# A split warm-up, an earlier block of normalisations and an earlier weight load in a fused attention and GEGLU kernel

## The chip, the cores and the metric

The kernel runs on one core of a Trainium2 chip. The core has five engines with a queue of instructions each: PE (TensorE, the matrix multiplier), DVE (VectorE), ACT (ScalarE), POOL (GpSimd) and SP (SyncE), which here only issues transfers (DMAs). Each queue is worked off in order; engines wait for one another through semaphores. The metric is the device time in microseconds; a lower number is better. The time before is 1046.27 us, the median of three runs (1045.1, 1046.27 and 1048.72 us).

## The reference

With x of 2048 tokens by 640 features, in float32:

```python
xn = layernorm(x)                                   # no scale, no bias
qkv = xn @ wqkv                                     # 32 heads of 20
scores = q @ k.T / sqrt(20)                         # causal, window of 256 tokens
A = softmax(scores) @ v @ wo
B = (gelu(xn @ w_gate) * (xn @ w_up)) @ w_down      # inner width 1728
out = x + A + B
```

## The kernel before

All matrix products are made from operands that are split in two: a high part (a copy rounded to the matrix format, made on ACT) and a low part (the rest, a subtraction on DVE or POOL). A product is then three matmuls, high by high, low by high and high by low. So nearly every tile goes through one ACT instruction and one DVE or POOL instruction before PE may use it.

The 2048 tokens are four chunks of 512, each of four tiles of 128 tokens. The work has these stages.

*Start* (lines 434 to 469). x is loaded a tile at a time (`ln_load`, L144, 320 KB each). DVE takes mean and variance (`ln_stats`, L149 to L151), makes the reciprocal deviations (L156 to L165) and normalises a tile in place (`ln_apply`, L169). PE transposes 128 by 128 blocks of it into PSUM (`turn`, L185), ACT copies the high part out (`xh`, L352 for the first chunk and L193 after), DVE subtracts the low part (`xl`, L349 and L194). While the first x tiles are under way PE runs 64 dummy matmuls of 128 by 128 by 128 on a tile of zeros (L444, `WARM = 64`), whose results are never read. The function `first_chunk` does chunk 0 in two halves of 256 tokens, in an order written out by hand (`manual_schedule` over PE, ACT, DVE and POOL); it also takes the statistics of the second chunk's four tiles (`xs[4]` to `xs[7]`, L421), makes two v tiles (`proj_v`, L322 and L108, in PSUM tile `ps_v`), normalises the second chunk's tiles (L426 to L431), and writes out the first q and k block (`save_qk`: ACT L277, DVE L273, ACT L255, POOL L259, then stores on SP at L268; the tile `r` between them has one buffer). Behind it chunks 1 to 3 follow (L455 to L469): `ln_turn`, then `proj_v` for four token tiles and `proj_qk` for one q and one k block (`ps_d`, L108). Outside the blocks ordered by hand a planner at build time orders each engine's queue by its own estimates, and it puts instructions from these chunks between those that are ordered by hand: in the trace the statistics of later tiles stand on DVE between two normalisations of the second chunk.

*Attention* (L818 to L871) from about 58 us to 543 us, with projections, v and the first gate and up tiles as filler matmuls; its order is by hand.

*Gate and up* (L1322 to L1412), `gate_up_pair` per tile f of 128 inner features, for two halves p of the tokens (`ps_g`, L972); by hand on all five engines. It has four hooks in each half, `more(0)` to `more(3)`, between its groups of matmuls, which run the lists `first` (half 0) and `second` (half 1). In the last tile (f = 12, `end`) these lists also prepare the down projection: `fetch` loads a quad of weights (two blocks of 128 rows of the down and output weights, 640 KB), `high_quad` (ACT, L1058) and `low_quad` (DVE, L1060 to L1062, recorded at L1077) split it. Quad 0 lands in the buffers `wr`, quad 1 (`fetch("b", 1, "at")`, L1043) in one of the three buffers with the tag `at`, which the jobs before (`Job`, L1079) used; quads 2 and 3 in buffers of the x sums. `load_step` loads the left operand of a step of the down projection (L1161 to L1171) and `split_step` splits it (`at`, L1186 to L1200).

*Down projection* (L1453 to L1484): 80 steps, ten per block of 256 tokens (`terms`, `ps`, L1244), `drain` (L1262) adds x and the results (L1267) and stores.

Of the kernel before, what the change touches and what calls it, by code (L numbers as in the profile page):

```python
# [39 lines left out]
HR = 5  # L40
NQD = 9
OWN = 4, 5
WARM = 64
XS0, XSN = 2, 3
HELD = 10, 11, 12
RAMP = 4.0
# [21 lines left out]
def block_kernel(ctx, tc, x, wqk, wv, wgu, wdo, wdl, out):  # L68
    nc = tc.nc
# [9 lines left out]
    ident = const.tile([128, 128], F32, name="ident")  # L79
# [88 lines left out]
    def ln_apply(xi, mv, rs):  # L168
        nc.vector.tensor_scalar(xi, xi, mv[:, 0:1], rs, op0=OP.subtract, op1=OP.mult)  # L169
# [62 lines left out]
    def load_qk(t):  # L232
        raw = wrp.tile([128, KT, 128], F32, name="wr", tag="wr")
        nc.sync.dma_start(raw, wqk[t])
        return raw
# [109 lines left out]
    def first_chunk(xs, wr0, wr5, prep, v0, lp):  # L345
        halves = slice(0, 256), slice(256, 512)

        def low(k, ps, cs):
            nc.vector.tensor_tensor(out=xl[:, k, cs], in0=ps, in1=xh[:, k, cs].bitcast(F32), op=OP.subtract)  # L349

        def high(k, ps, cs):
            nc.scalar.activation(xh[:, k, cs], ps, AF.Copy)  # L352

        def part(ps, w, r, cs, first=False, last=False, ks=range(KT)):
            for k in ks:
                nc.tensor.matmul(ps[:, cs], w[:, k, :], r[:, k, cs], start=first and k == 0,  # L356
                                 stop=last and k == KT - 1, skip_group_check=True)

        def high_qk(raw):
            wh = wp.tile([128, KT, 128], F32R, name="wqh", tag="wqh")  # L360
            nc.scalar.activation(wh, raw, AF.Copy)
            return wh

        def low_qk(raw, wh):
            wl = wp.tile([128, KT, 128], F32R, name="wql", tag="wql")
            nc.gpsimd.tensor_tensor(out=wl, in0=raw, in1=wh.bitcast(F32), op=OP.subtract)
            return wh, wl

        def hold(xi):
            nc.gpsimd.tensor_copy(one[:, 0:1], xi[:, 0:1])  # L370

        with tc.manual_schedule(engines=MANUAL | {mybir.EngineType.Pool}):
            mv = [lp.tile([128, 2, 2], F32, name="mv", tag="mv", bufs=2) for _ in range(2)]
            ln_stats(xs[0], mv[0][:, 0, :], lp)
            ln_stats(xs[1], mv[0][:, 1, :], lp)
            rs = ln_rstd(*ln_sqrt(mv[0], 2, lp), 2, lp)
            ln_apply(xs[0], mv[0][:, 0, :], rs[:, 0:1])
            ln_apply(xs[1], mv[0][:, 1, :], rs[:, 1:2])
            wh0 = high_qk(wr0)
            hold(xs[1])  # L380
            w0 = low_qk(wr0, wh0)
            ln_stats(xs[2], mv[1][:, 0, :], lp)
            ln_stats(xs[3], mv[1][:, 1, :], lp)
            ta = [turn(k, xs[0:2], "xmxmm"[k]) for k in range(KT)]
            dn = [psd.tile([128, C], F32, name="ps_d", tag="dn") for _ in range(2)]
            for k in range(4):
                high(k, ta[k], halves[0])
            vb = ln_sqrt(mv[1], 2, lp)
            high(4, ta[4], halves[0])
            wh5 = high_qk(wr5)  # L390
            rs = ln_rstd(*vb, 2, lp)
            ln_apply(xs[2], mv[1][:, 0, :], rs[:, 0:1])
            ln_apply(xs[3], mv[1][:, 1, :], rs[:, 1:2])
            hold(xs[3])
            w5 = low_qk(wr5, wh5)
            for ks_ in (range(4), (4,)):
                for n, w in enumerate((wh0, w0[1])):
                    part(dn[0], w, xh, halves[0], first=not n and not ks_[0], ks=ks_)
            part(dn[1], wh5, xh, halves[0], True)
            for k in range(KT):  # L400
                low(k, ta[k], halves[0])
            tb = [turn(k, xs[2:4], "oxmxm"[k]) for k in range(KT)]
            for k in range(KT):
                high(k, tb[k], halves[1])
            for k in range(KT):
                low(k, tb[k], halves[1])
            for _ in prep:
                pass
            v0 = v0[0]
            part(dn[0], wh0, xl, halves[0])  # L410
            part(dn[1], wh5, xl, halves[0])
            part(dn[0], wh0, xh, halves[1])
            part(dn[1], wh5, xh, halves[1])
            part(dn[0], w0[1], xh, halves[1])
            part(dn[0], wh0, xl, halves[1], last=True)
            part(dn[1], w5[1], xh, halves[0])
            part(dn[1], w5[1], xh, halves[1])
            part(dn[1], wh5, xl, halves[1], last=True)
            mv = lp.tile([128, 4, 2], F32, name="mv4", tag="mv4", bufs=2)
            for j in range(4):  # L420
                ln_stats(xs[4 + j], mv[:, j, :], lp)  # L421
            rs = ln_rstd(*ln_sqrt(mv, 4, lp), 4, lp)
            for i in range(2):
                for _ in proj_v(v0, i, (psm, "mx")):
                    pass
            ln_apply(xs[4], mv[:, 0, :], rs[:, 0:1])  # L426
            save_qk(0, 0, dn[0])
            ln_apply(xs[5], mv[:, 1, :], rs[:, 1:2])
            save_qk(5, 0, dn[1])
            for j in (2, 3):  # L430
                ln_apply(xs[4 + j], mv[:, j, :], rs[:, j:j + 1])  # L431
        return w0, w5, v0

    v0 = []
    with tc.tile_pool(name="lp", bufs=1, side="right") as lp:
        xs = [ln_load(t, lp) for t in range(2)]
        wr0 = load_qk(0)
        xs += [ln_load(t, lp) for t in (2, 3)]
        wr5 = load_qk(5)
        warm = lp.tile([128, 256], BF, name="warm")[:, 0:128]  # L440
        nc.vector.memset(warm, 0.0)
        ps = psd.tile([128, C], F32, name="ps_u", tag="dn")
        for i in range(WARM):
            nc.tensor.matmul(ps[:, 0:128], warm, warm, start=True, stop=True)  # L444
        prep = load_v(0, v0, lp, v_tiles())
        next(prep)
        xs += [ln_load(t, lp) for t in range(4, 8)]
        w0, w5, v0 = first_chunk(xs, wr0, wr5, prep, v0, lp)
        ones = lp.tile([4, 2 * C], BF, name="ones")
        nc.gpsimd.memset(ones, 0.0)  # L450
        nc.gpsimd.memset(ones[0:2], 1.0)
        for i in range(NK):
            for j in (0, 2):
                nc.sync.dma_start(ks[i][SR:64, j:j + 2].rearrange("p j t -> p (j t)"), ones)
        for c in range(1, NC):  # L455
            if c > 1:
                ln_scale(xs[4 * c:4 * c + 4], lp)
            ln_turn(4 * c, xs[4 * c:4 * c + 4])
            if c + 1 < NC:
                xs += [ln_load(t, lp) for t in range(4 * c + 4, 4 * c + 8)]  # L460
            if c == 1:
                for i in range(NQ):
                    for j in (0, 2):
                        nc.sync.dma_start(qs[i][SR + 2:64, j:j + 2].rearrange("p j t -> p (j t)"), ones[2:4])
            if c == 2:
                raws1 = [load_qk(1), load_qk(6)]
            if c < NC - 1:
                run(*[proj_v(v0, 4 * c - 4 + i, None if i % 2 else (psm, "mx")) for i in range(0 if c > 1 else 2, 4)])
                run(proj_qk(0, w0, c), proj_qk(5, w5, c))  # L469
# [890 lines left out]
    for j, f in enumerate(range(NFA, NF - 1)):  # L1360
        end = f + 1 == NF - 1
        first, second = {i: [] for i in range(4)}, {i: [] for i in range(4)}
# [22 lines left out]
        if not end:  # L1385
            for i, n in enumerate((1, 3, 1, 1) if j else (0, 2, 1, 1)):
                second[i].append(work(n))
        else:
            fetch("b", 0, "wr")
            raw13 = cp.tile([128, D], F32, name="raw13", tag="r13")  # L1390
            nc.sync.dma_start(raw13, wdl)
        gate_up_pair(f, w, 0, first)
        if end:
            assert not jobs and not going
            for n in range(2):
                load_step(n)
            fetch("b", 1, "at")

            def quad(q):
                high_quad("b", q)  # L1400
                low_quad("b", q)

            second[0].append(lambda: quad(0))
            second[0].append(lambda: [fetch("b", 2, "02"), fetch("b", 3, "03")])
            second[1].append(lambda: [split_step(0), load_step(2)])
            second[2].append(lambda: [split_step(1), quad(1), load_step(3)])
            second[3].append(lambda: [quad(2), split_step(2)])
# [47 lines left out]
    for n, (p, k) in enumerate(steps):  # L1455
        i = n % (NQD + 1)
        if i == 0:
            begun.clear()
            ps = {b: psn.tile([128, C], F32, name=f"ps_{b}", tag=f"b{b}") for b in (1, 2, 5, 3, 6, 4, 7, 8)}
# [68 lines left out]
```

## Time and profile before

| | |
|---|---|
| median of three runs | 1046.27 us |
| the profiled execution, time | 1045.72 us |
| its span, first to last instruction | 1044.0 us |
| outside the span | 1.72 us |
| PE busy | 1033.4 us |
| DVE, ACT, POOL busy | 741.7, 527.5, 385.5 us |

A line of the timeline gives the start, the length, the engine, the line of the program, the operation, output and input tiles, the shape and the count; in brackets stands how long the engine was idle before it and what ended that. PEld is the load of the stationary operand, which overlaps PE. Lengths of neighbouring matmuls overlap, since they are pipelined; the pace of a stream is read from the starts of its groups. A row of the windows gives the busy time and the count of instructions that touch the window. SPq and ACTq are the transfers that SP or ACT issues, with the time that the issue takes.

### The profile page before, as it was taken

How to read it: one execution, taken by the hardware profiler on the slowest of the kernel's cores; microseconds unless marked ns; L12 is line 12 of the kernel's file. 1: busy time of each engine (PE TensorE's matmuls, PEld its weight loads, DVE VectorE, ACT ScalarE, POOL GpSimd, SP SyncE). 2: the span in 40 equal slices, each digit the busy share in tenths (PEclk: the TensorE clock that was granted, in tenths of full speed). 3: DMA queues.
4: the chain of work that ended last, by engine and by line, in shares of the span. 5: the costliest groups of instructions: out<-in, count | busy, mean ns of one | idle time of the engine just before them, and what ended most of it. 6: DMA issues, size and time to landing. Idle time of an engine off the chain costs nothing.

```text
span 1044.0 us, 25563 instructions
## 1 busy us (share of the span) xinstructions
PE 1033.4 (99%) x9393; PEld 834.3 (80%) x9393; DVE 741.7 (71%) x2018; ACT 527.5 (51%) x1120; POOL 385.5 (37%) x623
## 2 busy tenths in 40 slices
PE   9999999999999999999999999999999999999998
PEld 8887666666777666666678888888888999999998
DVE  7755666677655676677736778776555889888887
ACT  4534766767666666666675322233224554433332
POOL 5122788888755787766461111101110000000000
PEclk9999999999999999999999999999999999999999
DMA  5552356554633354343325576662216874433333
GB/s 211 180 157 70 110 157 183 165 181 142 183 98 100 114 168 138 103 134 110 99 77 193 188 244 212 253 250 105 78 59 242 263 249 136 138 127 123 117 121 106
DMA packets 102150, 158.74 MB, mean 152 GB/s; under 512 B 14172, under 2 KB 55260, under 8 KB 102024
## 3 DMA queue, kind: packets, MB, share of 16 engines
q1 hardware_dynamic: 99640, 150.94, 44.5%
q10 hardware_dynamic: 2384, 6.16, 1.7%
q8 instruction: 74, 1.21, 0.5%
q14 instruction: 52, 0.43, 0.1%
HBM read 101.78 MB, written 54.92 MB: 150 GB/s over the span
## 4 chain that ended last, share of the span: by engine, by line
PE 90%; DVE 5%; ACT 2%; DMA 2%; issue 1%; POOL 0%; ACTq 0%; DVEq 0%; SPq 0%
PE ps_g L972 22%; PE ps_d L108 20%; PE ps L1244 20%; PE ps_e L572 8%; PE ps_v L108 7%; PE ps_o L615 5%; PE ps_m L507 5%; DVE junk L517 2%; PE ps_g L108 1%; DMA stg<-wdo 1%; ACT wb L1058 1%; PE ps_d L356 1%; PE ps_t L185 0%; DVE wb L1077 0%; DMA qs<-qd 0%
## 5 line engine op out<-in xcount | busy, mean ns | idle before, releaser
L517 DVE CUSTOM_DVE_ANT_0 junk<-ps_m,mask 128x320 bf16<-128x320 f32 (+2 forms) x512 | 243.0, 475 | 128.9 <-PE ps_m L507 71.0
L574 ACT ACTIVATE P<-ps_e 128x512 f32<-128x512 f32 (+2 forms) x384 | 198.7, 572 | 68.3 <-PE ps_e L572 67.8
L1244 PE MATMUL ps<-wb,at 128*128 128x320 f32 x999 | 156.4, 309 | 0.8 <-DVE xr L1267 0.8
L1244 PEld LDWEIGHTS ps<-wb,at 128*128 128x128 f32 x999 | 148.9, 188 | 1.5 <-issue 1.0
L587 POOL TENSOR_SCALAR_AFFINE_SELECT P<-P 128x256 f32<-128x256 f32 (+1 forms) x192 | 94.5, 494 | 73.2 <-ACT P L574 70.0
L572 PE MATMUL ps_e<-qs,ks 124*128 124x128 bf16 (+2 forms) x704 | 118.3, 278 | 0.1
L108 PE MATMUL ps_d<-xh,wqh 128*128 128x512 f32 x310 | 99.0, 422 | 0.2 <-ACT xh L193 0.2
L108 PE MATMUL ps_d<-xl,wqh 128*128 128x512 f32 x310 | 98.5, 422 | 0.0
L108 PE MATMUL ps_d<-xh,wql 128*128 128x512 f32 x310 | 97.6, 418 | 0.0
L101 POOL TENSOR_TENSOR wql<-wr,wqh 128x640 fp32r<-128x640 f32 x12 | 19.2, 1608 | 195.6 <-PE ps_g L972 171.1
L1244 PE MATMUL ps<-wt,at 128*128 128x320 f32 x552 | 88.9, 309 | 0.0
L572 PEld LDWEIGHTS <-ks 124*128 124x128 bf16 x704 | 49.5, 98 | 49.0 <-issue 33.4
L1244 PEld LDWEIGHTS ps<-wt,at 128*128 128x128 f32 x552 | 82.9, 188 | 0.1
L590 POOL TENSOR_SCALAR_AFFINE_SELECT P<-P 128x512 f32<-128x512 f32 (+1 forms) x144 | 76.7, 541 | 16.2 <-ACT P L574 16.2
L1198 ACT ACTIVATE at<-ss 128x512 fp32r<-128x512 f32 x59 | 37.3, 632 | 84.5 <-DVE ss L1077 84.5
L615 PE MATMUL ps_o<-P,v 64*32 64x320 f32 (+4 forms) x2816 | 74.2, 347 | 0.0
L259 POOL TENSOR_TENSOR pt<-r,pt 128x512 bf16<-128x512 f32 x40 | 46.8, 1169 | 64.6 <-ACT pt L255 57.0
L615 PEld LDWEIGHTS ps_o<-P,v 64*32 64x32 f32 x2816 | 50.8, 106 | 21.5 <-issue 0.9
L507 PE MATMUL ps_m<-ks,qs 60*64 60x320 bf16 (+3 forms) x1472 | 64.6, 260 | 3.4 <-DVE mx L517 1.5
L108 PEld LDWEIGHTS ps_d<-xh,wqh 128*128 128x128 f32 x310 | 56.0, 189 | 10.4 <-issue 1.6
L507 PEld LDWEIGHTS <-qs 60*64 60x64 bf16 x1472 | 29.1, 105 | 43.8 <-issue 35.6
L108 PEld LDWEIGHTS ps_d<-xh,wql 128*128 128x128 f32 x310 | 56.0, 189 | 10.1 <-issue 0.9
(195 smaller groups left out, 1967.4 us busy)
## 6 DMA issues: line engine op xcount, KB each, us to landing
hd<-he SPq DMA_DIRECT2D x50, 256.0 KB
hr<-hd SPq DMA_DIRECT2D x48, 256.0 KB
wr<-wgu SPq DMA_DIRECT2D x27, 320.0 KB
qs<-qd SPq DMA_DIRECT2D x64, 120.0 KB
ks<-kd SPq DMA_DIRECT2D x64, 120.0 KB
xi<-x SPq DMA_DIRECT2D x16, 320.0 KB
qs<-qd SPq DMA_DIRECT2D x64, 80.0 KB
ks<-kd SPq DMA_DIRECT2D x64, 80.0 KB
```

The source lines that it names most:

```text
L108: nc.tensor.matmul(ps, a(k), b(k), start=n == 0, stop=n == 3 * nk - 1)
L259: nc.gpsimd.tensor_tensor(out=pt[:, l, :], in0=r, in1=pt[:, 1, :], op=OP.subtract)
L507: nc.tensor.matmul(ps[64 * h:64 * h + 64, col:col + w], q[rows, j, q0:q0 + 64], ks_, start=True, stop=True, tile_position=(64 * r, 64 * h))
L517: nc.vector.tensor_tensor_reduce(out=junk[:, 0:n], in0=ps[:, 320 - n:320], in1=mask[:, 320 - n:320], scale=1.0, scalar=NEG, op0=OP.add, op ...
L572: nc.tensor.matmul(ps[:, col:col + n], k[0:QROWS, j, kc:kc + 128], q[0:QROWS, j, q0:q0 + n], start=True, stop=True)
L574: nc.scalar.activation(pt[:, j, lo:hi], ps[:, lo:hi], AF.Exp, scale=SCALE)
L587: nc.gpsimd.affine_select(out=a, in_=a, pattern=[[0, n], [1, 128]], compare_op=OP.is_ge, fill=0.0, base=0, channel_multiplier=-1)
L590: nc.gpsimd.affine_select(out=a, in_=a, pattern=[[0, n], [-1, 128]], compare_op=OP.is_ge, fill=0.0, base=-1, channel_multiplier=1)
L615: nc.tensor.matmul(os[r][32 * j:32 * j + 32, qa:qb], v[rows, w0_:w0_ + 32], pt[rows, j, col + qa - q0:col + qb - q0], start=r not in begun ...
L972: nc.tensor.matmul(ps, i, j, start=first and n == 0, stop=n == len(work) - 1, skip_group_check=True)
L1198: nc.scalar.activation(hi[:, 3:7], s, AF.Copy)
L1244: nc.tensor.matmul(ps[bank][:, 0:HD], *work[bank][j], start=bank not in begun, stop=final[p, bank] == n and j == len(work[bank]) - 1, skip ...
```

## The change

Three edits. First, the dummies go in two batches, 36 and 30, and in front of the second stands one transpose of the not yet normalised second x tile into the same PSUM tile; its result is not read either. Second, in `first_chunk` all four normalisations of the second chunk stand ahead of the first `save_qk`, where before the first stood ahead of it, the second between the two `save_qk`, and the third and fourth behind them. Third, the load of quad 1 is issued from the last hook of the first half of the last gate and up tile, where before it stood behind that half, its two stores and the first two `load_step`.

```diff
-WARM = 64
+WARM = 36, 30
...
-            ln_apply(xs[4], mv[:, 0, :], rs[:, 0:1])
+            for j in range(4):
+                ln_apply(xs[4 + j], mv[:, j, :], rs[:, j:j + 1])
             save_qk(0, 0, dn[0])
-            ln_apply(xs[5], mv[:, 1, :], rs[:, 1:2])
             save_qk(5, 0, dn[1])
-            for j in (2, 3):
-                ln_apply(xs[4 + j], mv[:, j, :], rs[:, j:j + 1])
...
-        for i in range(WARM):
-            nc.tensor.matmul(ps[:, 0:128], warm, warm, start=True, stop=True)
+        for i, n in enumerate(WARM):
+            if i:
+                nc.tensor.transpose(ps[:, 0:128], xs[1][:, 0:128], ident)
+            for _ in range(n):
+                nc.tensor.matmul(ps[:, 0:128], warm, warm, start=True, stop=True)
...
             nc.sync.dma_start(raw13, wdl)
+            first[3].append(lambda: fetch("b", 1, "at"))
         gate_up_pair(f, w, 0, first)
         if end:
             assert not jobs and not going
             for n in range(2):
                 load_step(n)
-            fetch("b", 1, "at")
```

## The prediction

> **What bounds the kernel.** I read the page first, then PE's waits, then the timeline at the three places that the change touches.
>
> ```profile
> span 1044.0 us, 25563 instructions
> PE 1033.4 (99%) x9393; PEld 834.3 (80%) x9393; DVE 741.7 (71%) x2018; ACT 527.5 (51%) x1120; POOL 385.5 (37%) x623
> PE 90%; DVE 5%; ACT 2%; DMA 2%; issue 1%; POOL 0%; ACTq 0%; DVEq 0%; SPq 0%
> ```
>
> PE is busy for 1033.4 of 1044.0 us and makes 90% of the chain that ended last. The change removes no matmul that the result needs, so it can only win from the 10.6 us in which PE is idle, and from hidden slack, where a pipelined matmul still counts as busy while the next one is late. The waits of PE, in the view of who waited for whom:
>
> ```profile
> PE ps_m L507 <- DVE mx L517: 1.5, 5, 0.4
> PE ps_u L444 <- DVE warm L441: 1.2, 1, 1.2
> PE ps_t L185 <- DVE xi L169: 0.9, 2, 0.5
> PE ps L1244 <- DVE xr L1267: 0.8, 1, 0.8
> ```
>
> The columns are total us, times and the longest. Two of these rows lie where the change works: PE's transposes wait for the normalisation (L169), 0.9 us in two places (one in the first chunk, one in the second), and the down projection waits once for a drain (L1267), 0.8 us. The other two lie in the attention and at the first dummy; the change reaches neither.
>
> **Edit 1, the dummies.** The timeline of the start, and the windows of the dummy's line (PE busy and count first, then PEld, clock and DMA):
>
> ```profile
> 1.17 6.18 PE L444 MATMUL ps_u<-warm 128*128 128x128 bf16 x64 [1.17 <-DVE warm L441]
> 4.75 0.49 DVE L149 BATCH_NORM_STATS2 st<-xi 128x6 f32<-128x320 f32 x1
> 7.03 1.14 DVE L169 TENSOR_SCALAR xi<-xi,mv,rs 128x640 f32<-128x640 f32 x2
> 7.79 1.63 PE L185 MATMUL ps_t<-ident,xi 128*128 128x128 f32 x10 [0.44 <-DVE xi L169]
> ...
> 5.50:6.00 0.50, 0.50 (x8) 0.50 (x6) 1.00 0.97 317
> 6.00:6.50 0.50, 0.50 (x9) 0.50 (x7) 1.00 0.91 317
> 6.50:7.00 0.50, 0.50 (x13) 0.50 (x11) 1.00 1.02 389
> ```
>
> The dummies end at 1.17 + 6.18 = 7.35; PE then waits 0.44 us until the first tile is normalised. The count per half microsecond jumps from 8 to 13 at about 6.3: the dummies run at one pace for 5.1 us and then at about twice it. With the pace doubled at 6.3 and a tail of 0.3 us, 64 dummies in 6.18 us give an estimate of 0.103 us each before it and 0.052 us after. The added transpose waits for the second tile; DVE began on that tile at 4.75 without a wait, so it had landed. The first 36 end at 1.17 + 36 x 0.103 = 4.88, so the transpose starts at once. PE has two dummies and one transpose more: 2 x 0.052 + 0.33 (the added one, with the semaphore, estimated from 1.63 us for ten and rounded up to twice that) = 0.44 us at most, which ends at 7.79, just when the first real transpose can start. Behind the new wait stand the 30 dummies and then the real transposes; DVE's in-place normalisation of the second tile now also waits for the transpose to have read it, which is over by 5.3, against 7.6. Cover: the 0.44 us of idle PE. If it were gone the cost would be those 0.44 us. If the tile landed later than 4.88, PE would idle for the difference instead of working through dummies of no use. I take 0; bounds -0.44 (the idle before the real transposes; nothing on PE can give more) and +1.5 (the rival on the pace, below).
>
> [...]
>
> **Edit 2, the second chunk.** The timeline from 21 to 41 us, DVE, then PE, then ACT:
>
> ```profile
> 21.31 0.61 DVE L169 TENSOR_SCALAR xi<-xi,mv,rs 128x640 f32<-128x640 f32 x1
> 23.49 0.49 DVE L149 BATCH_NORM_STATS2 st<-xi 128x6 f32<-128x320 f32 x1 [1.57 <-DMA xi<-x]
> 24.54 0.44 DVE L149 BATCH_NORM_STATS2 st<-xi 128x6 f32<-128x320 f32 x1
> 25.35 0.69 DVE L273 TENSOR_TENSOR r<-ps_d,pt 128x512 f32<-128x512 f32 x1 [0.37 <-issue]
> 28.59 1.13 DVE L169 TENSOR_SCALAR xi<-xi,mv,rs 128x640 f32<-128x640 f32 x2
> 37.15 0.60 DVE L169 TENSOR_SCALAR xi<-xi,mv,rs 128x640 f32<-128x640 f32 x1
> ...
> 22.48 0.90 PE L108 MATMUL ps_v<-wvh,xl 128*128 128x320 f32 x5
> 23.21 0.90 PE L108 MATMUL ps_v<-wvl,xh 128*128 128x320 f32 x5
> 23.94 0.60 PE L185 MATMUL ps_t<-ident,xi 128*128 128x128 f32 x4
> 29.25 0.66 PE L185 MATMUL ps_t<-ident,xi 128*128 128x128 f32 x4 [0.51 <-DVE xi L169]
> 36.73 1.30 PE L108 MATMUL ps_d<-xh,wql 128*128 128x512 f32 x5
> 37.86 1.30 PE L108 MATMUL ps_d<-xl,wqh 128*128 128x512 f32 x5
> 39.00 1.91 PE L185 MATMUL ps_t<-ident,xi 128*128 128x128 f32 x16
> ...
> 30.20 2.07 ACT L193 ACTIVATE xh<-ps_t 128x512 fp32r<-128x512 f32 x4 [0.86 <-PE ps_t L185]
> ```
>
> From 23.94 PE does the second chunk's 20 transposes, 30 `ps_v` and 30 `ps_d` matmuls, and reaches the third chunk's transposes at 39.00: 15.06 us. At full pace that work is 20 x 0.119 (1.91 / 16) + 30 x 0.146 (five from 22.48 to 23.21) + 30 x 0.226 (five from 36.73 to 37.86) = 2.4 + 4.4 + 6.8 = 13.6 us. So 1.47 us are lost there, of which 0.51 is the wait in the row at 29.25. The cause is on DVE: one normalisation at 21.31, then 1.57 us of waiting for a transfer that a later tile's statistics need, then the low part of `save_qk` at 25.35, and the last two normalisations only from 28.59. PE has the last tile's transposes after that, and ACT cannot start the high parts (each needs all four tiles) before 30.20.
>
> After: four normalisations from 21.31 at 0.55 us each end at 23.5, in what was the wait of 1.57 us, so they cost DVE nothing that it used. PE is free for transposes at 23.94 and no longer waits; ACT can begin the high parts at about 24.7, some 5.5 us sooner, while PE does the 30 `ps_v` matmuls. `save_qk` is not delayed: its DVE step waits for ACT and ran at 25.35, after 23.5. It issues no transfer sooner or later on SP but what follows from PE. What is late next is the third chunk: its last normalisation ran at 37.15 to 37.75, and PE now comes for it at 39.00 - 1.47 = 37.5. DVE has 1.65 us of normalising less to do in 25 to 30, which should bring it to about 36. ACT needs five high parts of 0.52 (2.07 / 4) besides the steps of `save_qk`, which wait for each other, so it may hold PE a little. I take -1.2 us; ends -1.47 (all of the loss) and +2.9 (the rival on DVE's order). PE is at full pace behind this stretch, so what is won stays won.
>
> **Edit 3, quad 1.** The transfers of SP (issues), then ACT, DVE and PE:
>
> ```profile
> 751.65 0.81 SPq L639 DMA_DIRECT2D wr<-wgu  x2
> 781.62 0.42 SPq L1391 DMA_DIRECT2D raw<-wdl  x1
> 791.34 0.93 SPq L1011 DMA_DIRECT2D hd<-he  x2
> 793.37 0.46 SPq L1043 DMA_DIRECT2D stg<-wdo  x1
> ...
> 800.67 1.28 ACT L1058 ACTIVATE wb<-stg 128x1280 fp32r<-128x1280 f32 x1 [3.42 <-DMA stg<-wdo]
> 801.98 1.49 DVE L1077 TENSOR_TENSOR wb<-stg,wb 128x1280 fp32r<-128x1280 f32 x1 [2.51 <-ACT wb L1058]
> 803.39 0.68 DVE L975 TENSOR_TENSOR hr<-ps_g,q 128x512 f32<-128x512 f32 x1
> 799.84 0.39 PE L972 MATMUL ps_g<-xl,s4h 128*128 128x512 f32 x1
> 835.36 1.68 DVE L1267 TENSOR_TENSOR xr<-ps,xr 128x320 f32<-128x320 f32 x4
> 835.99 4.19 PE L1244 MATMUL ps<-wb,at 128*128 128x320 f32 x27 [0.81 <-DVE xr L1267]
> ...
> 787.00:791.30 4.30, 4.30 (x21) 3.56 (x20) 1.97 (x4) 0.63 (x1) 0.00 (x0) 1.00 0.00 0
> ```
>
> The last row is a window, busy time of PE, PEld, DVE, ACT and POOL, clock, DMA share and rate: from 787.0 to 791.3 no transfer runs. Before, quad 1 was issued at 793.37, behind two stores and two loads of the same queue, and ACT waited 3.42 us for it, DVE in turn 2.51 us for ACT. DVE's next step, the sum of a group that PE had finished by 799.84 + 0.39 = 800.23, ran only at 803.39. After, the load stands in SP's queue behind the one at 781.62; SP has nothing to do between 782.0 and 791.34, so it is issued at about 782, unless its buffer is still held. The buffers with that tag belong to jobs, and SP's list from 751.65 to 781.62 has no transfer of a job, so they are free. It moves ahead of the two stores at 791.34 and the two loads, which it cannot delay, being issued 9 us before them; if the buffer were held to 791, SP would still be on time. The load lands well before 797.
>
> ACT then splits quad 1 at 800.67 - 3.42 = 797.25, DVE follows without its wait at 801.98 - 2.51 = 799.47 and ends at 800.96, and the sum runs there, 2.4 us sooner than at 803.39. That lead passes down DVE's queue to the drain at 835.36, for which PE waited 0.81 us at 835.99; one third of it is enough. I take -0.8 us. Ends: -0.81, as PE waits nowhere else in this stage, and 0, if the lead is eaten on the way by one of the weight loads that ACT issues later. A loss I exclude: nothing is put ahead of work that PE waits for.
>
> **Sum.** 0 - 1.2 - 0.8 = -2.0 us. The profiled execution took 1045.72 us (span 1044.0 and 1.72 around it), so 1043.7 us; that execution lies 0.55 under the median of the runs shown, so against the median this is 2.6 us less, against the like execution 2.0 us or 0.19%. I give 1043.7, since two of the three runs lie near the profiled one and the third (1048.72) above both.
>
> **Rivals.**
> *The warm-up steadies the start: 1043.0.* The runs before spread over 3.6 us (1045.1 to 1048.72). A dummy batch of fixed length covers one landing time of the x tiles only; if the later runs are those in which PE went idle ahead of its transposes and fell to the slow pace, the second batch mends that, and all runs come to the fastest less the two gains: 1045.1 - 2.0 = 1043.1, or 1042.8 at full gains. For it speaks the 0.44 us of slack in the row at 7.79; against it, that one profile shows no such run.
>
> *The gains are hidden anyway: 1045.7.* The chain of edit 3 is 33 us long and passes ACT's own weight loads, and the planner can reorder the second chunk so that ACT or the third chunk's normalisation gives the 1.5 us back. For it: only 1.25 us lie between 37.75 and 39.00. Against it: DVE has the room.
>
> *The planner puts statistics first (the slower end): 1047.8.* In the row at 23.49 a later tile's statistics stand ahead of a normalisation, waiting for a transfer. The planner could leave the statistics of three later tiles ahead of the last three normalisations, if it holds them ready. A tile's statistics take 24.54 - 23.49 = 1.05 us, so the last normalisation would end at 23.49 + 3 x 1.05 + 1.65 = 28.3, and PE, with its transposes lined up directly behind `ps_v`, would stand from 23.94: 4.4 us lost, less 1.47 and 0.8 won, so +2.1. With one tile ahead it comes out even, with two it is slower: that is the point from which it decides. Against it: four normalisations in a row leave DVE no gap in which the planner would look for other work.
>
> [...]
>
> **Numbers.** The bound for telling a difference is 0.3%, here 3.1 us, so faster means under 1043.13 and slower above 1049.41. The forecast has 0.47 (its own range 1042.9 to 1044.8; about a third of that lies under 1043.13), the steadier start 0.17, hidden gains 0.14, statistics first 0.13, the late pace 0.09. Faster: 0.17 and a third of 0.47, 0.33. Slower: half of the 0.13, where more than three tiles or the order further down is hurt, and some of the late pace and of what I have not seen, 0.11. The rest, 0.56, is within the bound. The range goes from 1042.0 (full gains on a start steadier than the fastest run by 0.8) to 1047.8 (statistics first).
>
> **What would show it.** Right: the first real transposes still at 7.8 with the dummies ending just ahead of them; four normalisations in one row from 21.3; the third chunk's 16 transposes at about 37.8 in place of 39.00; quad 1 issued at about 782 and neither ACT nor DVE waiting for it at about 797; no wait of PE for L1267. Wrong: PE waiting for a normalisation or a high part at 24 to 31, statistics between the normalisations, a low count of dummies per window beyond 6.5, or a total in which the second chunk's gain is seen at 38 us and gone by 62.

## The result and the profile after

The changed kernel takes 1044.32 us (median of 22 runs, 1042.95 to 1045.54), the kernel before on the same chip 1045.99 us (22 runs, 1043.41 to 1048.72). The ratio is 0.9984 with a 95% interval of 0.9977 to 0.9991: 1.67 us less, and less than the 0.3% that the prediction took as its bound, so no change by that bound. The spread of the runs, highest less lowest, fell from 5.3 to 2.6 us. The profiled execution took 1044.74 us.

The page of the changed kernel, with the lines that answer to those of before:

```profile
span 1043.0 us, 25570 instructions
PE 1031.9 (99%) x9396; PEld 833.9 (80%) x9396; DVE 741.3 (71%) x2018; ACT 528.0 (51%) x1120; POOL 384.5 (37%) x623
PE 93%; DVE 4%; ACT 1%; DMA 1%; issue 1%; POOL 0%; DVEq 0%; SPq 0%; ACTq 0%
```

PE's idle time has grown by 0.5 us (1043.0 less 1031.9 is 11.1, before it was 10.6), though the span is 1.0 us shorter. So PE gained in slack that counts as busy, and lost in plain waits. The waits of PE say where:

```profile
PE ps_t L185 <- DVE xi L169: 2.5, 4, 1.1
PE ps_m L508 <- DVE mx L518: 1.5, 5, 0.4
PE ps_u L445 <- DVE warm L439: 1.2, 1, 1.2
PE ps_t L185 <- DVE xl L194: 0.8, 2, 0.6
```

The wait for the drain (L1267 before, L1268 now) is gone. The wait of the transposes for the normalisation, which the change was to remove in the second chunk, has grown from 0.9 us in two places to 2.5 us in four. Of the 2.5 us, 1.10 lie ahead of the first real transpose, where the dummies now end sooner, and cost nothing; in the second chunk 0.51 us have become 1.05 (the rows at 7.71 and 25.42 below). The timeline of the start, PE, then POOL, SP and DVE:

```profile
1.17 3.57 PE L445 MATMUL ps_u<-warm 128*128 128x128 bf16 x36 [1.17 <-DVE warm L439]
4.63 0.30 PE L443 MATMUL ps_u<-ident,xi 128*128 128x128 f32 x1
4.76 1.84 PE L445 MATMUL ps_u<-warm 128*128 128x128 bf16 x30
7.71 0.33 PE L185 MATMUL ps_t<-ident,xi 128*128 128x128 f32 x1 [1.10 <-DVE xi L169]
25.42 2.46 PE L185 MATMUL ps_t<-ident,xi 128*128 128x128 f32 x16 [1.05 <-DVE xi L169]
39.39 1.91 PE L185 MATMUL ps_t<-ident,xi 128*128 128x128 f32 x16
...
10.95 0.94 POOL L452 MEMSET ones<- 2x1024 bf16 x1
4.08 2.71 SPq L144 DMA_DIRECT2D xi<-x  x4
11.91 5.17 SPq L455 DMA_DIRECT2D ks<-ones  x8
17.20 1.79 SPq L144 DMA_DIRECT2D xi<-x  x4
...
20.54 0.49 DVE L149 BATCH_NORM_STATS2 st<-xi 128x6 f32<-128x320 f32 x1 [0.70 <-DMA xi<-x]
21.76 0.44 DVE L149 BATCH_NORM_STATS2 st<-xi 128x6 f32<-128x320 f32 x1
23.73 0.49 DVE L149 BATCH_NORM_STATS2 st<-xi 128x6 f32<-128x320 f32 x1 [0.99 <-DMA xi<-x]
24.67 2.17 DVE L169 TENSOR_SCALAR xi<-xi,mv,rs 128x640 f32<-128x640 f32 x4
```

The four normalisations do stand in one row, but from 24.67 and not from 21.3: the statistics of three tiles of the third chunk stand ahead of them (the rows at 20.54, 21.76 and 23.73), two of which wait for their x tile. The third chunk's transposes come at 39.39, which is later than the 39.00 of before. At the other end of the kernel the rows of quad 1 (SP, ACT, DVE, PE):

```profile
782.44 0.42 SPq L1044 DMA_DIRECT2D stg<-wdo  x1
797.51 1.25 ACT L1059 ACTIVATE wb<-stg 128x1280 fp32r<-128x1280 f32 x1
799.73 1.49 DVE L1078 TENSOR_TENSOR wb<-stg,wb 128x1280 fp32r<-128x1280 f32 x1
801.13 0.68 DVE L976 TENSOR_TENSOR hr<-ps_g,q 128x512 f32<-128x512 f32 x1
817.67 27.59 PE L1245 MATMUL ps<-wb,at 128*128 128x320 f32 x187
```

The load is issued at 782.44, neither ACT nor DVE waits for it, the sum of the group runs at 801.13 in place of 803.39, and PE goes through 187 matmuls without the break that it had at 835.99.

### The profile page after: what moved, and what is told of

Its sections match the earlier page's. It is cut to its first block, busy times and chain, and to the rows that moved or that the text cites. A ratio compares the mean times of both kernels' runs of the same rounds, so it can differ in the third digit from the quotient of the medians.

```text
span 1043.0 us, 25570 instructions
## 1 busy us (share of the span) xinstructions
PE 1031.9 (99%) x9396; PEld 833.9 (80%) x9396; DVE 741.3 (71%) x2018; ACT 528.0 (51%) x1120; POOL 384.5 (37%) x623
## 4 chain that ended last, share of the span: by engine, by line
PE 93%; DVE 4%; ACT 1%; DMA 1%; issue 1%; POOL 0%; DVEq 0%; SPq 0%; ACTq 0%
PE ps_g L973 23%; PE ps L1245 23%; PE ps_d L108 20%; PE ps_e L573 8%; PE ps_v L108 6%; PE ps_o L616 5%; PE ps_m L508 5%; DVE junk L518 2%; PE ps_g L108 1%; DMA xi<-x 1%; PE ps_d L356 1%; DVE xl L194 0%; PE ps_t L185 0%; DVE st L149 0%; DVE st L150 0%
## 5 line engine op out<-in xcount | busy, mean ns | idle before, releaser
L108 PE MATMUL ps_d<-xl,wqh 128*128 128x512 f32 x310 | 98.5, 422 | 0.0
L108 PE MATMUL ps_d<-xh,wqh 128*128 128x512 f32 x310 | 98.2, 421 | 0.0
L108 PE MATMUL ps_d<-xh,wql 128*128 128x512 f32 x310 | 97.6, 419 | 0.0
L1002 ACT ACTIVATE hr<-hr 128x512 f32<-128x512 f32 x20 | 12.6, 632 | 102.0 <-DVE hr L976 102.0
L108 PEld LDWEIGHTS ps_d<-xh,wql 128*128 128x128 f32 x310 | 56.0, 189 | 10.1 <-issue 0.9
L108 PEld LDWEIGHTS ps_d<-xh,wqh 128*128 128x128 f32 x310 | 56.0, 189 | 9.7 <-issue 1.6
```

What stands on the lines that cost most here:

```text
L108: nc.tensor.matmul(ps, a(k), b(k), start=n == 0, stop=n == 3 * nk - 1)
```

## The experiments

The three edits were run alone and together, then edits 1 and 3 were varied. All times are medians in us; "start" is when the first gate and up matmul begins (`ps_g`, L108, the end of start and attention) and "rest" the time from there to the beginning of the last group of down matmuls, both from the timeline of each kernel's profile, so from one execution each. The ratio isn't the quotient of the two medians and differs from it by up to 0.11% (1.1 us, for the later quad 1).

| kernel | median (lowest to highest, runs) | before, same chip | ratio, 95% interval | start | rest |
|---|---|---|---|---|---|
| before | 1045.99 (1043.41 to 1048.72, 22) | | | 543.38 | 495.38 |
| all three edits | 1044.32 (1042.95 to 1045.54, 22) | 1045.99 | 0.9984 [0.9977, 0.9991] | 543.68 | 494.08 |
| the same again | 1044.04 (1043.02 to 1045.94, 11) | 1045.41 | 0.9992 [0.9983, 1.0001] | 542.79 | 495.05 |
| edit 1 alone | 1046.34 (1044.71 to 1048.77, 12) | 1045.40 | 1.0004 [0.9992, 1.0016] | 544.52 | 494.76 |
| edit 2 alone | 1044.08 (1042.60 to 1048.63, 12) | 1045.40 | 0.9993 [0.9980, 1.0006] | 542.24 | 496.00 |
| edit 3 alone | 1044.47 (1043.68 to 1045.20, 11) | 1045.40 | 0.9988 [0.9980, 0.9997] | 543.42 | 494.07 |
| edits 1 and 3 | 1045.34 (1044.57 to 1046.27, 11) | 1045.40 | 1.0002 [0.9993, 1.0011] | 544.26 | 494.22 |
| edits 2 and 3 | 1042.90 (1042.36 to 1044.67, 10) | 1045.09 | 0.9974 [0.9964, 0.9984] | 542.31 | 494.00 |
| the same again | 1042.87 (1042.36 to 1044.01, 11) | 1045.41 | 0.9981 [0.9972, 0.9990] | 541.27 | 494.06 |
| all three, split by a matmul | 1042.52 (1042.42 to 1044.37, 8) | 1045.09 | 0.9970 [0.9960, 0.9981] | 541.39 | 494.07 |
| the same again | 1042.85 (1042.35 to 1044.05, 11) | 1045.41 | 0.9977 [0.9969, 0.9986] | 541.38 | 494.38 |
| quad 1 still later | 1048.93 (1047.14 to 1050.06, 12) | 1045.09 | 1.0026 [1.0016, 1.0037] | 543.13 | 497.60 |
| split by a transpose of the identity | 1046.90 (1044.61 to 1049.11, 12) | 1045.09 | 1.0015 [1.0003, 1.0026] | 544.86 | 495.68 |

Four theories were to be told apart: that each edit does what the prediction's sum says; that the second batch steadies the start; that the break in the dummies puts off the fast pace; and, once edit 1 had been run alone, that it does harm through the order in which the planner puts the rest of the start, and not through PE's time.

**Edit 1 alone.**

```diff
-WARM = 64
+WARM = 36, 30
...
+            if i:
+                nc.tensor.transpose(ps[:, 0:128], xs[1][:, 0:128], ident)
```

> Edit 1 alone. Theory P (planner): the added transpose also moves the planner's order behind the start (statistics of the third chunk's tiles come ahead of the normalisations, as in the changed kernel, where the third chunk's transposes stood at 39.39 in place of 39.00), so the stretch up to 60 us becomes 0.3 to 1.2 us longer and the median is 1046 to 1047.2. Theory S (steadier start): the spread over the runs falls from the 5.3 us of before (1043.4 to 1048.7) to 2.6 us or less, and the median falls by 0.5 to 1 us, to about 1045.2, whatever the order. Both can hold; then the spread is small and the median near 1046.

1046.34 us, 0.94 us over before, though the interval of the ratio holds 1; the start ends 1.14 us later than before (544.52 against 543.38). DVE and PE of its timeline:

```profile
21.50 0.44 DVE L149 BATCH_NORM_STATS2 st<-xi 128x6 f32<-128x320 f32 x1
22.67 0.50 DVE L149 BATCH_NORM_STATS2 st<-xi 128x6 f32<-128x320 f32 x1 [0.20 <-DMA xi<-x]
23.62 0.60 DVE L169 TENSOR_SCALAR xi<-xi,mv,rs 128x640 f32<-128x640 f32 x1
...
40.61 1.25 PE L185 MATMUL ps_t<-ident,xi 128*128 128x128 f32 x10
```

The loss isn't at the dummies: the first real transposes start at 7.64. It is that the normalisation at 21.31 of the kernel before stands at 23.62 here, behind statistics of later tiles. An edit to PE's dummies has changed DVE's order 15 us later. Nor do the runs come together at the low end, as a steadier start would have them: the spread is 4.1 us and the median is not lower.

**Edit 2 alone.**

```diff
-            ln_apply(xs[4], mv[:, 0, :], rs[:, 0:1])
+            for j in range(4):
+                ln_apply(xs[4 + j], mv[:, j, :], rs[:, j:j + 1])
             save_qk(0, 0, dn[0])
-            ln_apply(xs[5], mv[:, 1, :], rs[:, 1:2])
...
```

> Edit 2 alone, with the order of the start as before. Theory P: four normalisations in one row from 21.3 to 23.5, the 16 transposes from 23.94, the third chunk's transposes at 37.5 to 37.8 in place of 39.00, median 1.2 to 1.47 us under before, about 1044.6, with the spread of before. Rival (nothing to win there): third chunk's transposes at about 39 as in the changed kernel and a median of 1046.

1044.08 us. The timeline is the one that the prediction described, POOL, SP, DVE, then PE:

```profile
14.35 0.94 POOL L449 MEMSET ones<- 2x1024 bf16 x1
4.08 5.68 SPq L144 DMA_DIRECT2D xi<-x  x5
15.31 5.18 SPq L452 DMA_DIRECT2D ks<-ones  x8
20.61 1.32 SPq L144 DMA_DIRECT2D xi<-x  x3
...
21.40 2.18 DVE L169 TENSOR_SCALAR xi<-xi,mv,rs 128x640 f32<-128x640 f32 x4
24.03 1.91 PE L185 MATMUL ps_t<-ident,xi 128*128 128x128 f32 x16
37.78 1.91 PE L185 MATMUL ps_t<-ident,xi 128*128 128x128 f32 x16
```

The normalisations run from 21.40, PE takes 16 transposes at one go, and the third chunk comes at 37.78, 1.22 us sooner than before; the start ends 1.14 us sooner. The interval of the ratio still holds 1, because the runs spread over 6.0 us. PE's wait for the drain, 0.8 us before, is 1.7 us in this execution, with quad 1 loaded at the same place of the program. Two of ACT's waits stand beside it:

```profile
PE ps L1242 <- DVE xr L1265: 1.7, 1, 1.7
...
797.50 1.28 ACT L1056 ACTIVATE wb<-stg 128x1280 fp32r<-128x1280 f32 x1 [1.24 <-DMA stg<-wdo]
831.73 1.27 ACT L1056 ACTIVATE wt<-stg 128x1280 fp32r<-128x1280 f32 x1 [3.55 <-DMA stg<-wtd]
```

ACT waited only 1.24 us for quad 1 here (3.42 before), but 3.55 us for a later quad of weights (1.41 before) shortly ahead of the drain. So the drain can be late by either load, and this longer wait isn't quad 1's.

**Edit 3 alone.**

```diff
             nc.sync.dma_start(raw13, wdl)
+            first[3].append(lambda: fetch("b", 1, "at"))
...
-            fetch("b", 1, "at")
```

> Edit 3 alone. Only the place of one load on SP changes. Forecast: ACT does not wait for quad 1, the wait of PE for the drain (0.81 us) is gone, median 0.8 us under before, about 1045.2, spread as before. Rival (hidden): the wait is gone but the time comes back before the end, median 1046.

1044.47 us, the drain's wait gone, the rest 494.07 us against 495.38. The runs spread over 1.5 us, where those of the kernel before, on the same chip, spread over 5.7 us (1043.56 to 1049.29). The start doesn't move (543.42), so the spread, which the prediction's first rival looked for in the start and which was expected here to stay as before, goes with the place of quad 1's load.

**Edits 1 and 3, without edit 2**.

```diff
-WARM = 64
+WARM = 36, 30
...
+            if i:
+                nc.tensor.transpose(ps[:, 0:128], xs[1][:, 0:128], ident)
...
+            first[3].append(lambda: fetch("b", 1, "at"))
...
-            fetch("b", 1, "at")
```

> Edits 1 and 3 without edit 2. Theory P: with the order that edit 1 brings, the four normalisations in a row are worth little or nothing, so this comes out within 0.5 us of the changed kernel, 1043.9 to 1044.9. Rival: edit 2 is worth its 1.2 us here too, and this is about 1045.5.

1045.34 us with a spread of 1.7 us: the steadiness of edit 3, and the late start of edit 1 (544.26). What edit 3 wins here edit 1 loses: 0.87 us over edit 3 alone, on the same chip. Theory P falls and its rival holds: edit 2 is worth about as much in the order that edit 1 brings (the changed kernel, taken on other chips, is 1.0 to 1.3 us faster).

**Edits 2 and 3, without edit 1**, run twice.

```diff
+            for j in range(4):
+                ln_apply(xs[4 + j], mv[:, j, :], rs[:, j:j + 1])
...
+            first[3].append(lambda: fetch("b", 1, "at"))
```

> Edits 2 and 3 without edit 1. Theory P (the split costs about 1 us, through the planner's order it brings): third chunk's transposes at 37.8 as with edit 2 alone, no wait of PE for the drain, median 1.1 + 0.9 us under before, about 1043.4, thus about 1 us under the changed kernel, and a spread of 1.5 to 2.6 us, as edit 3 alone has. Rival S (the split steadies the start): median no lower than the changed kernel's 1044.3 and a wider spread.

> Edits 2 and 3 without edit 1, beside the changed kernel. Theory P: 1.0 to 1.5 us under e9_changed_again, by the two profiles (third chunk's transposes at 37.75 against 39.39, start of the gate stage at 542.3 against 543.7). Rival S: equal to it.

1042.90 and 1042.87 us: both gains, and both kernels are beaten. The changed kernel was run again beside the second:

> The changed kernel as it is, beside the next two on the same chip. Theory P: 1.2 to 1.6 us under before, as in the first measurement, and 1.0 to 1.5 us over the next one.

It took 1044.04 us there, so leaving edit 1 out is worth 1.17 us, side by side. Its second profile has the same order of DVE's instructions with shorter waits for the x tiles (0.33 and 0.23 us in place of 0.70 and 0.99), the normalisations from 23.68 and the third chunk's transposes at 38.39, 1.00 us sooner than in the first profile and 0.6 to 0.7 us later than with edits 2 and 3 alone. It also shows that edit 3 doesn't rule the drain's wait out; PE's and ACT's waits in that profile:

```profile
PE ps L1245 <- DVE xr L1268: 0.8, 1, 0.8
...
ACT wt L1059 <- DMA stg<-wtd: 3.1, 1, 3.1
```

A later quad came late here (ACT waits 3.1 us for it), and the rest took 495.05 us, where the first profile had 494.08.

**Splitting by a matmul in place of the transpose.** All three edits, with a float32 matmul of the second x tile by itself between the two batches; its result, like that of the transpose, is not read. It keeps the wait for the tile and the two batches, and doesn't read the identity.

```diff
+            if i:
+                nc.tensor.matmul(ps[:, 0:32], xs[1][:, 0:128], xs[1][:, 0:32], start=True, stop=True)
```

> All three edits, but between the two batches stands a small float32 matmul of the second x tile with itself in place of the transpose. PE waits for the same tile, but the order of the other instructions is that of edits 2 and 3 alone. Its result is not read. Theory P: as e5_norms_load within 0.4 us, about 1043.4, as the split in itself is worth nothing. Rival S: lower than e5_norms_load by 0.5 us or with a clearly smaller spread. Rival C (the break costs time): higher by 0.5 us or more, about 1044.3.

> All three edits with the float32 matmul in place of the transpose, in the order of edits 2 and 3 alone. Theory P: within 0.3 us of e10_norms_load_again. Rival S (the split is worth something when it brings no new order): 0.4 us or more under it, as the medians of the first pair hinted (1042.5 against 1042.9).

1042.52 and 1042.85 us, against 1042.90 and 1042.87 us without edit 1 beside them. PE in the first of the two profiles:

```profile
1.18 4.02 PE L445 MATMUL ps_u<-warm 128*128 128x128 bf16 x36 [1.18 <-DVE warm L439]
4.99 0.58 PE L443 MATMUL ps_u<-xi 128*128 128x32 f32 x2
5.38 2.24 PE L445 MATMUL ps_u<-warm 128*128 128x128 bf16 x30
37.79 1.91 PE L185 MATMUL ps_t<-ident,xi 128*128 128x128 f32 x16
```

The third chunk comes at 37.79, as with edit 2 alone. So two batches with a wait between them cost nothing and win nothing that these runs resolve (0.0 to 0.4 us). The steadier start falls. So does the late pace as a cost: in this profile the first batch takes 4.02 us, against 3.57 in the changed kernel, and the second 2.24 us, against 1.84 in the second profile, so the second begins at the slow pace (by the prediction's estimates of 0.103 and 0.052 us for a dummy and 0.3 us of tail, 36 slow ones take 4.0 us and 30 fast ones 1.9), and the first real transposes still start at 7.80.

**The kernel before, with a transpose of the identity between the batches**, which waits for no x tile.

```diff
+            if i:
+                nc.tensor.transpose(ps[:, 0:128], ident, ident)
```

> Before, with the dummies in two batches of 36 and 30 and between them a transpose of the identity in place of the second x tile; no wait for x. The planner makes the same order of it as of edit 1. Theory P: as e1_split_only, third chunk's transposes at about 40.6, median about 1 us over before. Rival (the wait for x is what costs): as before, third chunk's transposes at 39.0.

1046.90 us, slower than before (1.0015, interval above 1). Its transposes of the second and third chunks fall into the same groups as those of edit 1 alone, and the third chunk's stand here:

```profile
40.81 1.25 PE L185 MATMUL ps_t<-ident,xi 128*128 128x128 f32 x10
```

That is 40.61 with edit 1 alone and 39.00 before. The x tile and the wait for it have no part in the loss; an early transpose that reads the identity is enough. With the matmul of the paragraph above neither the new order nor the loss appears, which leaves the order of the start as the cause.

**Quad 1 still later.** The kernel before with its load moved behind the four loads of quads 2 and 3.

```diff
-            fetch("b", 1, "at")
...
-            second[0].append(lambda: [fetch("b", 2, "02"), fetch("b", 3, "03")])
+            second[0].append(lambda: [fetch("b", 2, "02"), fetch("b", 3, "03"), fetch("b", 1, "at")])
```

> Before, with the load of quad 1 put behind the four loads of quads 2 and 3, some 2 us later. Theory Q (the landing of quad 1 sets the drain of the first block and makes the spread): ACT waits 5 us or so for quad 1 in place of 3.42, PE waits 2 to 3 us for the drain in place of 0.81, median 1 to 2 us over before, about 1047, and a spread as wide as before's or wider. Rival (the spread comes from elsewhere): median within 0.4 us of before.

1048.93 us, 3.8 us more than before. The timeline of SP and ACT, then PE's waits:

```profile
795.05 0.42 SPq L1043 DMA_DIRECT2D stg<-wdo  x1
802.50 1.27 ACT L1058 ACTIVATE wb<-stg 128x1280 fp32r<-128x1280 f32 x1 [5.76 <-DMA stg<-wdo]
```

```profile
PE ps L1244 <- DVE xr L1267: 1.2, 1, 1.2
PE ps L1244 <- DVE wb L1077: 0.4, 1, 0.4
PE ps L1244 <- DVE w L1077: 0.3, 1, 0.3
PE ps L1244 <- DVE at L1077: 0.3, 1, 0.3
```

A load issued 1.68 us later (795.05 against 793.37) holds ACT for 5.76 us in place of 3.42, and PE waits at four places instead of one, 2.2 us in all. The rest takes 497.60 us against 495.38, 2.2 us of the 3.8; the profiled execution, 1047.80 us, is one of the shorter ones of this kernel. The median rose more than was expected, and the spread, 2.9 us, is smaller than the 4.65 us of before beside it, not as wide.

## Why the prediction was right or wrong

**The total.** 1043.7 was forecast and 1044.32 measured; against the kernel before, -2.0 in the sum and -1.67 between the medians, -0.98 between the two profiled executions. It is close, but partly by luck: by the starts and rests of the profiles edit 1 cost 1.5 us where 0 was forecast, and edits 2 and 3 won 1.6 and 1.2 us where 1.2 and 0.8 were forecast, so the misses are of opposite sign.

**Edit 1, costed at 0: the step that failed.** The working named what stands behind the new wait on PE and the tile's normalisation on DVE, and found all of it covered. That was right as far as it went: the dummies end at 4.76 + 1.84 = 6.60, PE then waits 1.10 us for the normalisation, and the first real transposes start at 7.71, as before. The batches even proved shorter than estimated, because the fast pace came before the second one: the dummies touching half a microsecond go from 7 (3.5 to 4.0 us) to 11 (4.0 to 4.5), and the second batch starts at 4.76. What was left out is that the order of the start isn't fixed: a planner orders what isn't ordered by hand, as the section on the kernel before says, and the prediction used that only against edit 2. The rows show the chain. The second memset of `ones` moves on POOL from 14.35 (edit 2 alone) to 10.95; SP's eight transfers from `ones` start at 11.91 in place of 15.31, ahead of the ninth x tile, which is now issued at 17.20 with the three behind it. With edit 2 alone the row at 4.08 has five loads, the ninth tile's among them, ahead of `ones`; here it has four. DVE waits for that tile, and the statistics of two more tiles have moved ahead of the normalisations. By the table the order costs 1.2 us without edit 2 (the mean start of edit 1, edits 1 and 3, and the identity is 544.55, that of before, edit 3 and the later quad 543.31) and 1.5 us with it (543.24 over two profiles, against 541.72 over five). The starts within such a group lie up to 1.0 us apart, so these are good to some half a microsecond. Medians taken on one chip say a little less: 0.94 us (edit 1 against before), 0.87 (edits 1 and 3 against edit 3) and 1.17 (all three against edits 2 and 3). The bound of +1.5 held it, by another mechanism: no run shows the late pace from which the 1.5 us came, and in the changed kernel the second batch ran its 30 dummies in 1.84 us.

**Edit 2, -1.2: right.** Its loss of 1.47 us comes out as 1.51 when the three products aren't rounded, which changes nothing. In the old order it brings the third chunk 1.22 us sooner and the start of gate and up from 543.31 to 541.72, 1.6 us by means of profiles and 1.32 us by the medians. In the order that edit 1 makes it is still worth 1.3 us (544.55 to 543.24). That is why the changed kernel's start ends near that of before, not 1.2 us ahead of it: two terms of the same size cancel. Of the signs listed as wrong, the profile shows PE waiting for a normalisation (1.05 us at 25.42) and statistics of two more later tiles, ahead of the four normalisations though not between them; edit 2 alone brings neither.

**Edit 3, -0.8: right, a little small.** Issue, waits and the sum 2.26 us sooner came as worked out. The rest takes 494.24 us in the mean of the eight profiles with the edit and 495.46 us in the four without it that load quad 1 at the old place, 1.2 us less; the end of -0.81 counted only the plain wait for the drain. It missed that the price of the old place varies: the wait of ACT for this load is 3.42 us before, 0.91 with edit 1, 1.24 with edit 2, 2.81 with the identity. One profile gave one draw of it. Nor does the rest follow this wait alone: it is longest with edit 2 (496.00), where a later quad held ACT for 3.55 us. Its own caution, that a later weight load can eat the lead, came true in one of two profiles of the changed kernel.

**The rivals.** The steadier start has its result, a narrower spread, and the wrong cause: kernels with edit 3 spread over 1.5 to 2.9 us, those with the old place over 4.1 to 6.0, whatever was done to the dummies (and the one with the still later place over 2.9, from 1047.14 up). Nor did the first ten real transposes run slower where PE stood idle ahead of them: they took 1.63 us behind 0.44 us of idle (before), 0.27 (edit 2 alone) and 0.18 (split by a matmul), and 1.64 us behind none (the later quad 1). The late pace (the break in the dummies putting off the fast one), for which no run shows a ground, didn't come: the second batch ran 30 dummies in 1.84 us at once, and in 1.84 to 1.88 us in all other profiles with a transpose between the batches, where 30 at the slow pace would take 3.4 us (an estimate: 30 x 0.103 and the tail of 0.3). "Statistics first" happened in a mild form, at a price of 1.2 to 1.5 us instead of 4.4, and not through the edit that it was charged to. Hidden gains happened nowhere: with edits 2 and 3 both arrive at the end in full (1042.9).

**What stays open.** That a transpose among the dummies which reads the identity goes with the new order is shown by four kernels with it and by the matmul without it. Whether it is the read of the identity or the kind of instruction wasn't told apart, and why the planner answers so wasn't tried. Nor is it shown what makes quad 1, or the later quad, land sooner or later from run to run.

## What to carry to other kernels

Before an added instruction is costed at nothing because its engine is idle, ask whether a planner orders the other engines: here one added transpose, whose result isn't read, went with another order, and the loss stood on other queues, 15 us away. When runs of one kernel spread, find which edit narrows the spread; here a load moved ahead of a stretch without transfers (issued at 782.13 us; none from 787.0 to 791.3 in the kernel before) took 0.9 us off the median and 4.1 us off the longest run (of 11 runs, against 35 of the kernel before). And split a change into its parts even when its total comes out as forecast: here leaving one of the three parts out was worth another 1.2 us.

## What the runs showed of the hardware

**Normalisation beside a memset.** The pair of normalisations at about 11.4 us takes 1.14 us in the kernel before, where POOL's second memset of `ones` runs only at 14.25, and 1.14 too with edit 2 alone, the split by a matmul and the later quad 1 (memset at 14.35, 14.35 and 14.19). In the changed kernel, where the memset runs at 10.95, it takes 1.40: 0.88 the first of the two and 0.60 the second, against 0.61 each before. With edits 1 and 3 (memset at 10.97) it takes 1.40 as well. In the changed kernel, and below it with edit 1 alone:

```profile
11.36 1.40 DVE L169 TENSOR_SCALAR xi<-xi,mv,rs 128x640 f32<-128x640 f32 x2
```

```profile
10.88 0.94 POOL L454 MEMSET ones<- 2x1024 bf16 x1
11.52 1.17 DVE L169 TENSOR_SCALAR xi<-xi,mv,rs 128x640 f32<-128x640 f32 x2
```

The memset ends at 11.89 in the first (10.95 + 0.94), 0.53 us into the pair, which is 0.26 longer than before; in the second it ends at 11.82, 0.30 us in, and the pair is 0.03 longer. In both the pair grows by 0.27 us less than it overlaps. The memset wasn't moved by itself, so that it is the memset that lengthens the pair is argued and not shown.

**The pace of the dummies.** The 64 dummies took 6.18 us before and 5.08 with edit 3 alone, whose start is the same program:

```profile
1.17 5.08 PE L444 MATMUL ps_u<-warm 128*128 128x128 bf16 x64 [1.17 <-DVE warm L441]
7.79 1.63 PE L185 MATMUL ps_t<-ident,xi 128*128 128x128 f32 x10 [1.53 <-DVE xi L169]
```

The first real transposes start at 7.79 in both, since the normalisation sets them. In the kernel before a dummy is 314 ns long up to about 6.3 us and 219 ns behind it, with a granted clock of 1.00 on both sides; in the changed kernel the same step, from 311 to 219 ns, comes at about 4.0 us. So the step comes at another time in another execution: the same 64 dummies took 1.10 us less in the second profile, 6.45 us with edit 2 alone and 6.51 with the later quad 1. What sets its time isn't shown. It cost nothing here.
